# The 64-row remainder of a 576-deep contraction, run as pairs of 64-row array tiles in both gMLP input projections

## The chip, the cores and the metric

The kernel runs on one core of one Trainium2 chip. The metric is the device time of one execution in microseconds (us), and lower is better. A profile's span is the same execution seen by the profiler from the first to the last instruction; it is 1 to 2 us shorter than the time. A few words used throughout: a bank is a piece of PSUM, the memory into which TensorE writes; a chunk is a slice of the contraction, 128 deep (the last one 64), and a unit is a slice of the output columns. PE is TensorE's matrix multiply, PEld its weight load, DVE is VectorE, ACT is ScalarE, POOL is GpSimd and SP is SyncE.

## The reference, cut to what matters

Four layers run in the order A, B, A, B on x of 2048 rows and D = 576 columns. Layer A is local attention with 32 heads, layer B a gMLP. The change is in layer B, and in the layernorm that feeds both kinds.

```python
def _B_ref(x, w_in, w_sp, b_sp, w_out):          # x: (1, 2048, 576); w_in: (576, 4608)
    Fh = w_in.shape[-1] // 2                      # 2304
    z = _gelu(jnp.einsum('bsd,df->bsf', x, w_in)) # both input projections, 576 deep
    z1 = z[..., :Fh].copy()
    z2 = _layernorm(z[..., Fh:], axis=-1)
    g = jnp.einsum('ts,bsf->btf', w_sp, z2) + b_sp[None, :, None]
    return jnp.einsum('bsf,fd->bsd', z1 * g, w_out)
# ...
x = x + _A_ref(_layernorm(x, axis=-1), A_wqkv, A_wo)
x = x + _B_ref(_layernorm(x, axis=-1), B_w_in, B_w_sp, B_b_sp, B_w_out)
# ... and both once more
```

The contraction of both input projections is 576 = 4 x 128 + 64 deep. The second half of `w_in` ("win2" below) makes z2, the first half ("w1") makes z1.

## The kernel before: the parts that matter

The kernel runs the 64-row remainder as a fifth 128-deep matmul in which rows 64 to 127 of the weights are zeros. So it costs as much as a full one: ten w1 matmuls, two of them remainders, take 2.16 us, 216 ns each (chain of waits below).

The normalised rows are written into a buffer of 640 columns, whose last 64 columns were zeroed once, and a DMA transpose puts them into `xnT` as five chunks of 128 partitions.

```python
        for b in self.xn_bufs:
            nc.gpsimd.memset(b[:, D:640], 0.0)
# ...
    def ln_xn(self, x_t, nrows, mv, rstd, nmr, eng="act"):
        # ...
        if eng == "act":
            nc.scalar.activation(out=xn[:nrows, 0:D], in_=x_t[:nrows, :], func=ACT.Identity,
                                 scale=rstd[:nrows, 0:1], bias=nmr[:nrows, 0:1])
        else:
            e = nc.gpsimd if eng == "pool" else nc.vector
            e.tensor_scalar(out=xn[:nrows, 0:D], in0=x_t[:nrows, :], scalar1=mv[:nrows, 0:1],
                            scalar2=rstd[:nrows, 0:1], op0=ALU.subtract, op1=ALU.mult)
        return xn
```

The win2 projection of layer B, for each of 16 blocks of 128 rows: five units (four of 512 columns, one of 256), five chunks each.

```python
        nc.vector.memset(win2b[64:128, 4 - NPF, :].bitcast(i32), 0)
        # ... weights arrive by DMA; chunks 0 to NPF-1 are already resident, the others come late
        def p1_main(i):
            # ...
            if i == 0:
                order = [(u, c) for c in range(NPF) for u in units] + [(u, c) for u in units for c in range(NPF, 5)]
            else:
                order = [(u, c) for u in units for c in range(5)]
            for ((ci, c0, sub, w), c) in order:
                nc.tensor.matmul(pzvs[ci][:, sub * 512:sub * 512 + w], lhsT=self.xnT[:, c, PADL + i * P:PADL + (i + 1) * P],
                                 rhs=win2(c)[:, c0 + sub * 512:c0 + sub * 512 + w],
                                 start=(c == 0), stop=(c == 4))
            # ... gelu on ACT, sum of squares on DVE and ACT, then p1_norm: six slices on DVE, three on POOL
```

The w1 projection with the gating, for each of 18 groups of 128 columns per layer (9 weight blocks x 2), so 36 groups in all:

```python
        for jj in range(NB):
            w1 = p2.tile([P, 5, 256], bf16, name="w1")
            nc.gpsimd.memset(w1[64:128, 4, :], 0.0)
            for c in range(5):
                kc = 128 if c < 4 else 64
                self.dma(w1[:kc, c, :], self.B_w_in[c * P:c * P + kc, jj * 256:(jj + 1) * 256], eng=nc.sync)
            # ...
            for sub in range(2):
                z1T = p2.tile([P, S], bf16, name="z1T")
                for q2 in range(0, NQ, 2):
                    # ...
                    for qq in range(nq2):
                        for c in range(5):
                            nc.tensor.matmul(pz1[:, qq, :], lhsT=w1[:, c, sub * P:(sub + 1) * P],
                                             rhs=self.xnT[:, c, PADL + (q2 + qq) * 512:PADL + (q2 + qq + 1) * 512],
                                             start=(c == 0), stop=(c == 4))
                    # ... gelu on ACT
                for q in range(NQ):
                    pg = self.PT_tile([P, 512], f32, "pg")
                    for i in range(NS):
                        nc.tensor.matmul(pg[:, :], lhsT=z2b[jj][:, i, sub * P:(sub + 1) * P],
                                         rhs=W_sb[:, i, q * 512:(q + 1) * 512],
                                         start=(i == 0), stop=(i == NS - 1))
                    # ... add the bias and multiply by z1T on DVE
```

The softmax here doesn't subtract the row's maximum and nothing guards it: scores larger than these inputs give would overflow.

Of the kernel before, what the change touches and what calls it, by code (L numbers as in the profile page):

```python
# [10 lines left out]
ACT = mybir.ActivationFunctionType  # L11
# [4 lines left out]
i32 = mybir.dt.int32  # L16
# [3 lines left out]
P = 128  # L20
D = 576
# [6 lines left out]
PADL = HALO  # L28
# [33 lines left out]
class K:  # L62
# [24 lines left out]
    def setup(self):  # L87
        nc, tc, cfg, ctx = self.nc, self.tc, self.cfg, self.ctx
# [3 lines left out]
        c = self.consts  # L92
# [32 lines left out]
        for b in self.xn_bufs:  # L125
            nc.gpsimd.memset(b[:, D:640], 0.0)
# [45 lines left out]
    def ln_xn(self, x_t, nrows, mv, rstd, nmr, eng="act"):  # L172
        nc = self.nc
        xn = self.xn_bufs[self.xn_rr % len(self.xn_bufs)]
        self.xn_rr += 1
        if eng == "act":
            nc.scalar.activation(out=xn[:nrows, 0:D], in_=x_t[:nrows, :], func=ACT.Identity,
                                 scale=rstd[:nrows, 0:1], bias=nmr[:nrows, 0:1])
        else:
            e = nc.gpsimd if eng == "pool" else nc.vector  # L180
            e.tensor_scalar(out=xn[:nrows, 0:D], in0=x_t[:nrows, :], scalar1=mv[:nrows, 0:1],  # L181
                            scalar2=rstd[:nrows, 0:1], op0=ALU.subtract, op1=ALU.mult)
        return xn
# [15 lines left out]
    NPF = 3  # L199
# [548 lines left out]
    def layer_B(self, li):  # L748
        nc, tc, cfg = self.nc, self.tc, self.cfg
        S, NS, Fh, NJ, NB, NQ = cfg.S, cfg.NS, cfg.Fh, cfg.NJ, cfg.NB, cfg.NQ  # L750
# [12 lines left out]
        NPF = self.NPF  # L763
# [4 lines left out]
        nc.vector.memset(win2b[64:128, 4 - NPF, :].bitcast(i32), 0)  # L768
        for c in range(NPF, 5):
            kc = 128 if c < 4 else 64  # L770
            self.dma(win2b[:kc, c - NPF, :], self.B_w_in[c * P:c * P + kc, Fh:2 * Fh], eng=(nc.sync, nc.scalar)[c % 2])

        def win2(c):
            return win2a[:, c, :] if c < NPF else win2b[:, c - NPF, :]
# [5 lines left out]
        c0 = 0  # L780
# [9 lines left out]
        def p1_main(i):  # L790
            zp = p1.tile([P, Fh], bf16, name="zp", bufs=2)
            sums = p1.tile([P, ncch + 2], f32, name="z_sums", bufs=3)
            pzvs = []
# [13 lines left out]
            if i == 0:  # L807
                order = [(u, c) for c in range(NPF) for u in units] + [(u, c) for u in units for c in range(NPF, 5)]
            else:
                order = [(u, c) for u in units for c in range(5)]  # L810
            for ((ci, c0, sub, w), c) in order:
                nc.tensor.matmul(pzvs[ci][:, sub * 512:sub * 512 + w], lhsT=self.xnT[:, c, PADL + i * P:PADL + (i + 1) * P],  # L812
                                 rhs=win2(c)[:, c0 + sub * 512:c0 + sub * 512 + w],
                                 start=(c == 0), stop=(c == 4))
# [66 lines left out]
        for jj in range(NB):  # L881
            w1 = p2.tile([P, 5, 256], bf16, name="w1")
            nc.gpsimd.memset(w1[64:128, 4, :], 0.0)
# [5 lines left out]
            for sub in range(2):  # L889
                z1T = p2.tile([P, S], bf16, name="z1T")  # L890
                for q2 in range(0, NQ, 2):
                    nq2 = min(2, NQ - q2)
                    pz1 = self.H_tile("pz1")
                    for qq in range(nq2):
                        for c in range(5):
                            nc.tensor.matmul(pz1[:, qq, :], lhsT=w1[:, c, sub * P:(sub + 1) * P],
                                             rhs=self.xnT[:, c, PADL + (q2 + qq) * 512:PADL + (q2 + qq + 1) * 512],
                                             start=(c == 0), stop=(c == 4))
                    nc.scalar.activation(out=z1T[:, q2 * 512:(q2 + nq2) * 512],
                                         in_=pz1[:, 0:nq2, :].rearrange("p a b -> p (a b)"), func=ACT.Gelu_apprx_tanh)  # L900
# [154 lines left out]
```

## Time and profile before

| | before |
|---|---|
| time, median of 3 runs | 1349.56 us (1348.8 to 1353.09) |
| span of the profile | 1348.4 us |
| PE busy | 1249.9 us, 93% of the span |
| share of PE in the chain of waits that ended last | 62% |
| stage (a), w1 and gating, from the last normalised slice to the first output matmul | 325.7 and 321.5 us in the two B layers |
| one round of a w1 group and its 64 `pg` matmuls | 18.130 us |
| stage (b), win2 with gelu and layernorm: one block | 5.01 us |

The page of the profile gives the busy time of each engine and, in its part 4, the chain that ended last.

```profile
PE 1249.9 (93%) x8656; PEld 659.5 (49%) x8656; DVE 616.5 (46%) x1402; ACT 384.2 (28%) x595; POOL 356.4 (26%) x487
PE 62%; DVE 11%; POOL 10%; issue 7%; DMA 6%; ACT 3%; SPq 1%; ACTq 0%; POOLq 0%; DVEq 0%
```

PE is busy nearly all the time, but only 62% of the chain is PE: in the rest of the time some other engine decides when things go on, although PE has work in between. So the average says little, and the kernel has to be read stage by stage. The table of busy time by stretches does that. This is the kernel before over one pass of stage (b) and one of stage (a); the columns are the stretch, its length, the busy time of each engine with its instructions, PE's granted clock, the share of the DMA engines, and GB/s.

```profile
core 0: us, PE busy (x) PEld busy (x) DVE busy (x) ACT busy (x) POOL busy (x), PEclk, DMA share, GB/s
190.00:286.00 96.00, 87.04 (x430) 41.35 (x427) 67.97 (x210) 55.81 (x129) 69.73 (x85) 1.00 0.56 122
286.00:607.00 321.00, 318.31 (x1474) 144.13 (x1474) 99.49 (x145) 36.87 (x36) 3.57 (x10) 1.00 0.03 9
```

In the second stretch, stage (a), PE is busy 318 of 321 us and nothing else is near a limit: a matmul saved there is time saved. In the first, stage (b), no engine is full. The chain of waits in stage (a) of the kernel before (start, length, what):

```profile
297.07 2.16 PE pz_4181 L896 x10
299.23 2.16 PE pz_4193 L896 x10
301.39 13.81 PE pg L904 x64
315.20 2.16 PE pz_4294 L896 x10
```

Ten w1 matmuls take 2.16 us, so one 512-column matmul takes 216 ns, and the 64 `pg` matmuls say the same (13.81 / 64). One round is 315.20 - 297.07 = 18.13 us.

The Trainium skill, "TensorE: Matmul & The Clock Gate", section "Back-to-back issue gap", gives 131 ns for a sustained stream of 512-column matmuls with weight loads between them, and 216 ns for isolated ones. This trace is such a stream, with a weight load for each matmul (1474 of each in the second stretch above), and shows 216 ns. The measurement decides here: a matmul removed from stage (a) is worth 216 ns.

In stage (b) the timeline (start, length, engine, line, operation, and in brackets the idle time before it and what ended it) shows a loop. These lines are of the kernel before, one block and the start of the next:

```profile
228.25 1.02 ACT L816 ACTIVATE zp<-pz 128x1024 bf16<-128x1024 f32 x1 [1.55 <-POOL z2b_3101 L845]
...
231.10 2.13 POOL L845 TENSOR_SCALAR z2b_3101<-zp,z_rstd,z_nmr 128x256 bf16<-128x256 bf16 x1
231.10 1.77 DVE L819 CUSTOM_DVE_ANT_0 z_junkD<-zp 128x1536 bf16<-128x1536 bf16 x1
...
233.26 1.02 ACT L816 ACTIVATE zp<-pz 128x1024 bf16<-128x1024 f32 x1 [1.56 <-POOL z2b_3101 L845]
```

The first gelu of each block waits 1.55 us for POOL's last normalised slice, and the next block starts 233.26 - 228.25 = 5.01 us later. PE's work per block is 20 x 0.216 + 5 x 0.109 = 4.86 us, less than the period: PE waits for ACT to free its output banks.

### The profile page before, as it was taken

What the parts mean: (1) busy time and instruction counts of PE and PEld (TensorE: products, weight loads), DVE (VectorE), ACT (ScalarE), POOL (GpSimd) and SP (SyncE); (2) the same over time, 40 slices, a digit from 0 to 9 for tenths busy, and PEclk for the clock granted to TensorE, in tenths of its full rate; (3) what the DMA queues carried; (4) which work ended last, traced back from release to release, by engine and by line L of the source; (5) the groups of instructions that cost most, each with busy time, mean ns of one, the idle gap of its engine ahead of it and who ended that gap; (6) DMA issues with size and microseconds to landing.
All of it is one profiled execution on the core that took longest, in us unless ns stands there. A gap on an engine that the chain in (4) does not pass through costs nothing.

```text
span 1348.4 us, 21451 instructions
## 1 busy us (share of the span) xinstructions
PE 1249.9 (93%) x8656; PEld 659.5 (49%) x8656; DVE 616.5 (46%) x1402; ACT 384.2 (28%) x595; POOL 356.4 (26%) x487
## 2 busy tenths in 40 slices
PE   1999969989999999998998987899999999999997
PEld 0456644434444444445754655444444444444576
DVE  4468858843322332332534878588323223333221
ACT  2556726620011111001126665465101111100000
POOL 7445547830000000002141646488000000000111
PEclk9999989999999999997999999899999999999999
DMA  9449759020000000009653677861100000000232
GB/s 264 98 94 145 121 134 214 1 90 6 9 10 9 10 9 9 0 4 266 179 137 62 151 145 129 181 125 41 43 9 9 10 9 9 2 7 1 72 113 67
DMA packets 180128, 101.04 MB, mean 75 GB/s; under 512 B 138276, under 2 KB 162212, under 8 KB 180028
## 3 DMA queue, kind: packets, MB, share of 16 engines
q1 hardware_dynamic: 170208, 84.15, 28.1%
q10 hardware_dynamic: 6364, 8.55, 2.2%
q0 software_dynamic: 3456, 6.96, 2.2%
q8 instruction: 68, 1.11, 0.3%
q14 instruction: 32, 0.26, 0.1%
HBM read 41.16 MB, written 16.52 MB: 43 GB/s over the span
## 4 chain that ended last, share of the span: by engine, by line
PE 62%; DVE 11%; POOL 10%; issue 7%; DMA 6%; ACT 3%; SPq 1%; ACTq 0%; POOLq 0%; DVEq 0%
PE pg L904 36%; PE po L941 9%; DVE z_junkD L819 4%; PE pp L412 3%; DMA QK<-stg 2%; POOL ln_xn_84 L181 2%; POOL ln_xn_81 L181 1%; POOL ln_rstd L164 1%; POOL z_rstd L835 1%; POOL ln_xn_83 L181 1%; POOL ln_xn_82 L181 1%; DMA wout_b<-in_B_w_out_dram 1%; DMA wv_sb<-in_A_wqkv_dram 1%; DMA win2b<-in_B_w_in_dram 1%; DVE z_msq L828 1%
## 5 line engine op out<-in xcount | busy, mean ns | idle before, releaser
L908 DVE TENSOR_TENSOR g_tmp<-pg,bsp 128x512 f32<-128x512 f32 x144 | 99.4, 692 | 435.5 <-PE pg L904 423.9
L412 PE MATMUL pp<-xnT,wqk_sb 128*128 128x512 bf16 x400 | 100.7, 394 | 29.8 <-DMA xnT<-ln_xn_84 28.5
L812 PEld LDWEIGHTS <-xnT 128*128 128x128 bf16 x800 | 78.4, 98 | 97.0 <-issue 13.0
L812 PE MATMUL pz<-win2a,xnT 128*128 128x512 bf16 x384 | 103.1, 379 | 5.9 <-ACT zp L816 4.4
L164 POOL TENSOR_TENSOR ln_rstd<-ln_rstd,neg_half 112x1 f32<-112x1 f32 (+2 forms) x70 | 43.4, 621 | 152.3 <-DVE ln_rstd L163 152.1
L812 PE MATMUL pz<-win2b,xnT 128*128 128x512 bf16 x256 | 77.0, 386 | 6.9 <-DMA win2b<-in_B_w_in_dram 6.9
L816 ACT ACTIVATE zp<-pz 128x1024 bf16<-128x1024 f32 x64 | 65.0, 1020 | 44.6 <-POOL z2b_9746 L845 18.9
L412 PEld LDWEIGHTS <-wqk_sb 128*128 128x128 bf16 x400 | 36.9, 100 | 71.2 <-issue 36.0
L819 DVE CUSTOM_DVE_ANT_0 z_junkD<-zp 128x1536 bf16<-128x1536 bf16 x32 | 56.9, 1777 | 18.7 <-ACT zp L816 18.7
L370 PE MATMUL pv<-wv_sb,xnT 128*128 128x288 bf16 (+1 forms) x380 | 62.2, 286 | 0.2 <-DVE stg L418 0.2
L76 POOL DMA_DIRECT2D wout_b<-in_B_w_out_dram x14 | 7.5, 541 | 172.4 <-PE pg L904 172.4
L76 POOL DMA_DIRECT2D QK<-stg x52 | 31.5, 608 | 73.0 <-ACT stg L420 28.0
L584 DVE TENSOR_TENSOR x_new<-pw,xo 112x288 f32<-112x288 f32 (+1 forms) x76 | 33.5, 445 | 18.0 <-PE pw L582 10.7
L420 ACT CAST stg<-pp 128x512 bf16<-128x512 f32 x54 | 31.0, 585 | 37.4 <-PE pp L412 22.7
L370 PEld LDWEIGHTS <-xnT 128*128 128x128 bf16 (+1 forms) x380 | 33.5, 97 | 15.8 <-issue 1.4
L489 PE MATMUL L_ps<-QK 18*128 18x112 bf16 (+1 forms) x1216 | 32.0, 210 | 4.9 <-DMA QK<-stg 1.7
L418 DVE CAST stg<-pp 128x512 bf16<-128x512 f32 x26 | 18.0, 691 | 37.0 <-PE pp L412 33.5
L159 DVE BATCH_NORM_STATS2 ln_st<-x_new 112x6 f32<-112x288 f32 (+1 forms) x76 | 33.9, 449 | 1.2
L489 PEld LDWEIGHTS <-QK 18*128 18x128 bf16 (+1 forms) x1216 | 20.4, 93 | 25.6 <-issue 21.6
L845 POOL TENSOR_SCALAR z2b_3101<-zp,z_rstd,z_nmr 128x256 bf16<-128x256 bf16 x16 | 32.4, 2024 | 0.0
L845 POOL TENSOR_SCALAR z2b_9746<-zp,z_rstd,z_nmr 128x256 bf16<-128x256 bf16 x16 | 32.4, 2023 | 0.0
L904 PE MATMUL pg<-W_sb,z2b_3093 128*128 128x512 bf16 x128 | 28.4, 379 | 1.9 <-DVE z2b_3093 L848 1.9
(549 smaller groups left out, 2513.3 us busy)
## 6 DMA issues: line engine op xcount, KB each, us to landing
xres_73<-x_new SPq DMA_DIRECT2D x18, 252.0 KB
xo<-xres_74 SPq DMA_DIRECT2D x18, 252.0 KB
xres_75<-x_new SPq DMA_DIRECT2D x18, 252.0 KB
QK<-stg POOLq DMA_DIRECT2D x52, 72.0 KB, 3.8
win2a<-in_B_w_in_dram SPq DMA_DIRECT2D x2, 1728.0 KB
QK<-stg SPq DMA_DIRECT2D x48, 72.0 KB
wqk_sb<-in_A_wqkv_dram ACTq DMA_DIRECT2D x4, 576.0 KB
out_dram<-ob SPq DMA_DIRECT2D x16, 144.0 KB
```

Source lines behind the costliest of these rows:

```text
L164: nc.gpsimd.tensor_tensor(out=rstd[:nrows, :], in0=rstd[:nrows, :], in1=self.neg_half[:nrows, :], op=ALU.pow)
L181: e.tensor_scalar(out=xn[:nrows, 0:D], in0=x_t[:nrows, :], scalar1=mv[:nrows, 0:1], scalar2=rstd[:nrows, 0:1], op0=ALU.subtract, op1=ALU.mult)
L370: nc.tensor.matmul(pv[:nk, 0:288], lhsT=self.xnT[:, c, QT * t:QT * t + nk], rhs=wv_sb[:, c, hh * 288:(hh + 1) * 288], start=(c == 0), stop ...
L412: nc.tensor.matmul(pp[:, :], lhsT=wqk_sb[:, c, wc0:wc0 + P], rhs=self.xnT[:, c, col0:col0 + 512], start=(c == 0), stop=(c == 4))
L489: nc.tensor.matmul(L_ps[:nk, j, ftl * QT:ftl * QT + nq], lhsT=kT[32 * j:32 * j + DH, g, QT * t:QT * t + nk], rhs=qT[32 * j:32 * j + DH, g, ...
L812: nc.tensor.matmul(pzvs[ci][:, sub * 512:sub * 512 + w], lhsT=self.xnT[:, c, PADL + i * P:PADL + (i + 1) * P], rhs=win2(c)[:, c0 + sub * 5 ...
L816: nc.scalar.activation(out=zp[:, c0:c0 + cn], in_=pzvs[ci][:, 0:cn], func=ACT.Gelu_apprx_tanh, accum_out=sums[:, ci:ci + 1])
L819: nc.vector.tensor_tensor_reduce(out=junkD[:], in0=zp[:, 0:SQ_D], in1=zp[:, 0:SQ_D], scale=1.0, scalar=0.0, op0=ALU.mult, op1=ALU.add, acc ...
L845: nc.gpsimd.tensor_scalar(out=z2b[b][:, i, :], in0=zp[:, b * 256:(b + 1) * 256], scalar1=rstd[:, 0:1], scalar2=nmr[:, 0:1], op0=ALU.mult, ...
L904: nc.tensor.matmul(pg[:, :], lhsT=z2b[jj][:, i, sub * P:(sub + 1) * P], rhs=W_sb[:, i, q * 512:(q + 1) * 512], start=(i == 0), stop=(i == ...
L908: nc.vector.tensor_tensor(out=tmp[:], in0=pg[:, :], in1=bsp[:, q * 512:(q + 1) * 512], op=ALU.add)
L941: nc.tensor.matmul(acc[hh], lhsT=uT[j // 2][:, j % 2, i * P:(i + 1) * P], rhs=wout_j(j)[:, hh * 288:(hh + 1) * 288], start=(j == 0), stop= ...
```

## The change

The intent is to split the array into two tiles of 64 rows that work side by side (`tile_position` in the code names the tile). Then two 64-deep remainders, of two different output units, should take the time of one full matmul. One tile takes its operands from partitions 0 to 63 and the other from 64 to 127. So the weights' 64 rows are loaded twice by DMA, and each normalised tile carries its last 64 columns twice, by a small copy before the transpose. The zeroing falls away. The order of the matmuls is changed so that the remainders of a group stand together: two units' full chunks, then all remainders, then the other units' full chunks.

```diff
-        for b in self.xn_bufs:
-            nc.gpsimd.memset(b[:, D:640], 0.0)
@@ ln_xn @@
+            nc.scalar.copy(out=xn[:nrows, D:640], in_=xn[:nrows, 512:D])
         else:
             # ...
+            e.tensor_copy(out=xn[:nrows, D:640], in_=xn[:nrows, 512:D])
@@ layer_B, win2 @@
-        nc.vector.memset(win2b[64:128, 4 - NPF, :].bitcast(i32), 0)
+        self.dma(win2b[64:128, 4 - NPF, :], self.B_w_in[512:576, Fh:2 * Fh], eng=nc.scalar)
@@ p1_main @@
-            # ... the order of before, resident chunks first in block 0
+            def z_full(us, cs):
+                # ... full chunks of units us, start=(c == 0), stop=False
+            def z_half(us):
+                for u in us:
+                    ci, c0, sub, w = units[u]
+                    r = 64 * (u % 2)
+                    nc.tensor.matmul(pzvs[ci][:, sub * 512:sub * 512 + w],
+                                     lhsT=self.xnT[r:r + 64, 4, PADL + i * P:PADL + (i + 1) * P],
+                                     rhs=win2(4)[r:r + 64, c0 + sub * 512:c0 + sub * 512 + w],
+                                     start=(u >= 2), stop=(u < 2), tile_position=(r, 0))
+            z_full(range(2), range(4))
+            z_half(range(nu))
+            # ... then chunks 0 to 3 of units 2, 3, 4
@@ layer_B, w1 @@
-            nc.gpsimd.memset(w1[64:128, 4, :], 0.0)
+            self.dma(w1[64:128, 4, :], self.B_w_in[512:576, jj * 256:(jj + 1) * 256], eng=nc.sync)
@@ w1 group @@
+                def z1_half(q, first):
+                    r = 64 * (q % 2)
+                    nc.tensor.matmul(pz1s[q // 2][:, q % 2, :], lhsT=w1[r:r + 64, 4, sub * P:(sub + 1) * P],
+                                     rhs=self.xnT[r:r + 64, 4, PADL + q * 512:PADL + (q + 1) * 512],
+                                     start=first, stop=not first, tile_position=(r, 0))
+                z1_full(0, True)
+                z1_full(1, True)
+                for q in range(NQ):
+                    z1_half(q, q >= 2)
+                z1_full(2, False)
+                z1_full(3, False)
```

More of the change, by code (lines that the diff above doesn't have):

```diff
@@ L806, in p1_main @@
                     units.append((ci, c0, sub, w))
-            if i == 0:
-                order = [(u, c) for c in range(NPF) for u in units] + [(u, c) for u in units for c in range(NPF, 5)]
-            else:
-                order = [(u, c) for u in units for c in range(5)]
-            for ((ci, c0, sub, w), c) in order:
-                nc.tensor.matmul(pzvs[ci][:, sub * 512:sub * 512 + w], lhsT=self.xnT[:, c, PADL + i * P:PADL + (i + 1) * P],
-                                 rhs=win2(c)[:, c0 + sub * 512:c0 + sub * 512 + w],
-                                 start=(c == 0), stop=(c == 4))
+            def z_full(us, cs):
+                for u in us:
+                    ci, c0, sub, w = units[u]
+                    for c in cs:
+                        nc.tensor.matmul(pzvs[ci][:, sub * 512:sub * 512 + w],
+                                         lhsT=self.xnT[:, c, PADL + i * P:PADL + (i + 1) * P],
+                                         rhs=win2(c)[:, c0 + sub * 512:c0 + sub * 512 + w],
+                                         start=(c == 0), stop=False)
+            def z_half(us):
+                for u in us:
+                    ci, c0, sub, w = units[u]
+                    r = 64 * (u % 2)
+                    nc.tensor.matmul(pzvs[ci][:, sub * 512:sub * 512 + w],
+                                     lhsT=self.xnT[r:r + 64, 4, PADL + i * P:PADL + (i + 1) * P],
+                                     rhs=win2(4)[r:r + 64, c0 + sub * 512:c0 + sub * 512 + w],
+                                     start=(u >= 2), stop=(u < 2), tile_position=(r, 0))
+            nu = len(units)
+            z_full(range(2), range(4))
+            z_half(range(nu))
+            for u in range(2, nu):
+                ci, c0, sub, w = units[u]
+                for c in range(4):
+                    nc.tensor.matmul(pzvs[ci][:, sub * 512:sub * 512 + w],
+                                     lhsT=self.xnT[:, c, PADL + i * P:PADL + (i + 1) * P],
+                                     rhs=win2(c)[:, c0 + sub * 512:c0 + sub * 512 + w],
+                                     start=False, stop=(c == 3))
             for ci, (c0, cn) in enumerate(cchunks):
@@ L890, in layer_B, with z1_full @@
                 z1T = p2.tile([P, S], bf16, name="z1T")
-                for q2 in range(0, NQ, 2):
-                    nq2 = min(2, NQ - q2)
-                    pz1 = self.H_tile("pz1")
-                    for qq in range(nq2):
-                        for c in range(5):
-                            nc.tensor.matmul(pz1[:, qq, :], lhsT=w1[:, c, sub * P:(sub + 1) * P],
-                                             rhs=self.xnT[:, c, PADL + (q2 + qq) * 512:PADL + (q2 + qq + 1) * 512],
-                                             start=(c == 0), stop=(c == 4))
-                    nc.scalar.activation(out=z1T[:, q2 * 512:(q2 + nq2) * 512],
-                                         in_=pz1[:, 0:nq2, :].rearrange("p a b -> p (a b)"), func=ACT.Gelu_apprx_tanh)
+                pz1s = [self.H_tile("pz1") for _ in range(NQ // 2)]
+                def z1_full(q, first):
+                    for c in range(4):
+                        nc.tensor.matmul(pz1s[q // 2][:, q % 2, :], lhsT=w1[:, c, sub * P:(sub + 1) * P],
+                                         rhs=self.xnT[:, c, PADL + q * 512:PADL + (q + 1) * 512],
+                                         start=(first and c == 0), stop=(not first and c == 3))
+                def z1_half(q, first):
[9 more added lines that the diff above has]
+                z1_full(3, False)
+                for q2 in range(0, NQ, 2):
+                    nc.scalar.activation(out=z1T[:, q2 * 512:(q2 + 2) * 512],
+                                         in_=pz1s[q2 // 2][:, :, :].rearrange("p a b -> p (a b)"), func=ACT.Gelu_apprx_tanh)
                 for q in range(NQ):
```

## The prediction

> **What bounds the kernel now.** The table of busy time by stretches shows three kinds of stage. (a) Gating with the w1 projection (286 to 607, 948 to 1266 us): PE is busy 318 of 321 us. The chain of waits repeats: two pieces of ten w1 matmuls, 2.16 us each, then 64 `pg` matmuls, 13.81 us; a 512-column matmul costs 216 ns. (b) The win2 projection with gelu and layernorm (190 to 286, 850 to 948 us): the timeline repeats every 5.01 us. PE needs 20 x 0.216 + 5 x 0.109 = 4.86 us, but ACT's gelu waits 1.56 us for POOL's last normalised slice, and DVE (`z_junkD` 1.77 us plus six slices) and POOL (2.12 us for that slice) feed each other in a loop that sets the period. (c) Attention: POOL waits 2.9 us per tile for DVE; PE does not bind.
>
> **Removed.** Per w1 group two 512-column passes (432 ns), per win2 block also two; the fifth, 256-column unit has no partner.
>
> **Added: switches between full array and row tiles.** The Trainium skill, "TensorEngine Tiling (Array Packing)", Key Properties, says that changing tiling mode drains TensorE. The trace agrees in attention's 18-row tiles: from the start of a 512-column matmul to the first tile takes 312 ns instead of 216, from a 288-column one 218 instead of 122, from the last 112-column tile to the full array 140 instead of about 47. So about 95 ns per switch, 190 a round trip. Row tiles do overlap: 16 tiles of 112 columns start within 195 ns, four passes.
> w1 group: 4.32 us before; after 16 x 0.216 + 2 x 0.216 + 0.02 + 0.19 = 4.10 us. Gain 0.22 us, x36 = 7.9 us, all critical.
> win2 block: the instruction order puts four halves together and the fifth elsewhere, so two round trips: -0.43 + 0.38 = -0.05 us of PE, off the critical path.
>
> **Losses (estimates from the trace).**
> - Start of (b): the first block no longer runs all resident chunks first. PE waits there for win2b already (3.6 and 2.9 us), and a table load (1.28 us) hides part. A third win2b transfer and a later last transpose: 0.7 us x2.
> - Start of (a): a sixth w1 transfer goes first in its queue; an issue takes 0.47 us (five: 2.35): 0.5 us x2.
> - 64-column copies: ACT about 0.22 us (256 columns take 0.38, 1024 take 1.02), POOL about 0.3 us (1 column 0.27, 256 columns 0.6). In the first layer's head and at last tiles: 1 us; by contention on DVE 0.5 us.
> Together about 4 us. The removed memsets were hidden.
>
> **Predicted time:** 1349.6 - 7.9 + 4 = about 1345 us, range 1340 to 1352. Faster by over 2%: 0.01; within: 0.97; slower by over 2%: 0.02.
>
> **What the profile would show.** Each w1-plus-`pg` round shrinks from 18.13 to about 17.91 us; the second half of a pair starts within about 20 ns of the first; about 310 ns from the last full matmul to the first half. (b)'s 5.01 us and attention's 5.8 us per tile stay.
>
> **What would make it wrong.** If the halves don't overlap, 0.43 us more per group turn the gain into an 8 us loss. If 64-row tiles switch more cheaply, the gain is up to 15 us. If POOL's copies stretch DVE in attention (36 tiles), some us are lost. If the new order in (b) makes PE wait for PSUM buffers, its period grows, x32 blocks.

## The result, and the profile after

Ratios in this document are computed as the mean time of one kernel's fast runs over the mean of the other's fast runs of the same rounds, so they are not quite the ratios of the medians quoted beside them. Brackets after a ratio are its 95% interval.

| | before | after |
|---|---|---|
| median of the runs of this comparison | 1351.07 us (1348.8 to 1353.09, 4 runs) | 1343.91 us (1342.94 to 1345.92, 4 runs) |
| ratio, after over before | | 0.9957 [0.9935, 0.998] |
| span of the profile | 1348.4 us | 1341.8 us |
| round of a w1 group and 64 `pg` | 18.130 us | 17.910 us |
| block of stage (b) | 5.01 us | 5.01 us |

The changed kernel is correct and 0.4% faster, which is "within 2%". The prediction was 1345 us in a range of 1340 to 1352.

```profile
PE 1243.5 (93%) x8656; PEld 636.1 (47%) x8656; DVE 614.1 (46%) x1400; ACT 391.4 (29%) x622; POOL 362.6 (27%) x508
```

PE has as many matmuls as before (a remainder is still one instruction) and 6.4 us less busy time. The chain of waits in stage (a) of the changed kernel:

```profile
973.27 1.73 PE pz L914 x8
975.00 0.54 PE pz L920 x4
975.54 1.83 PE pz L914 x8
977.37 13.81 PE pg L935 x64
```

The four remainders, line 920, take 0.54 us from the first one's start to the start of the next full matmul, instead of 4 x 0.216 = 0.86 us. The whole group is 4.10 us instead of 4.32. The timeline shows the starts of the same group's records (a record's length includes the matmul's own latency, so starts are what is compared):

```profile
973.11 1.89 PE L914 MATMUL pz<-xnT,w 128*128 128x512 bf16 x8
974.93 0.60 PE L920 MATMUL pz<-xnT,w 64*128 64x512 bf16 x4
975.47 1.90 PE L914 MATMUL pz<-xnT,w 128*128 128x512 bf16 x8
```

Inside these groups the records' starts repeat to 1 or 2 ns in all rounds: from the last full matmul to the first remainder 312 ns, to its pair partner 3 ns, to the next pair 223 ns, and from the last remainder to the next full matmul 308 ns. A full matmul follows another after 216 ns. So a change of the array's mode costs 312 - 216 = 96 ns on the way in and 308 - 216 = 92 ns on the way out, about 0.19 us for the round trip, and the pairs overlap fully.

These are prices; what fills the 96 ns the runs do not settle. The changed kernel's trace adds one hint. Inside a stream a weight load is recorded 2 ns after the start of the previous matmul, some 214 ns ahead of its own. At the switch the first remainder's load is recorded 308 ns after the start of the last full matmul and only 4 ns ahead of its own. So no load runs ahead across the switch here, and no run here separates the lost lead of the load (it takes 92 ns itself) from an emptying of the array.

The Trainium skill, "TensorEngine Tiling (Array Packing)", Key Properties, says that changing the tiling mode drains TensorE but gives no figure; these 96 and 92 ns are this kernel's figure. "TensorE: Matmul & The Clock Gate", Part 3, puts the tiles of a pack about 4 ns apart at issue; the trace has 3 ns.

In stage (b) the same lines as before, in the changed kernel:

```profile
224.68 1.02 ACT L835 ACTIVATE zp<-pz 128x1024 bf16<-128x1024 f32 x1 [1.56 <-POOL z2b L864]
...
227.67 0.61 PE L820 MATMUL pz<-win2b,xnT 64*128 64x512 bf16 x4
228.11 0.27 PE L820 MATMUL pzs<-win2b,xnT 64*128 64x256 bf16 x1
...
229.70 1.02 ACT L835 ACTIVATE zp<-pz 128x1024 bf16<-128x1024 f32 x1 [1.56 <-POOL z2b L864]
...
230.86 0.81 PE L811 MATMUL pz<-win2a,xnT 128*128 128x512 bf16 x3 [0.21 <-ACT zp L835]
```

All five remainders of the block stand together (lines at 227.67 and 228.11), with one round trip through the modes. PE's work is 16 x 0.216 + 4 x 0.109 for the full chunks, 2 x 0.216 + 0.109 for the remainders and 0.19 for the switches, 4.62 us instead of 4.86. But the gelu still waits 1.56 us for POOL and comes 229.70 - 224.68 = 5.02 us after the last one, and what PE saved turns into a wait of its own: the idle 0.21 us before the next block, for ACT. The 0.24 us are saved off the critical path, in the 28 of 32 blocks whose remainders stand together, and are worth nothing.

At the start of stage (b) time was lost. The first block of the first B layer, before and then after:

```profile
188.06 1.02 PE L812 MATMUL pz<-win2a,xnT 128*128 128x512 bf16 x4 [0.99 <-DVE x_new L584]
...
195.01 1.68 PE L812 MATMUL pz<-win2b,xnT 128*128 128x512 bf16 x7 [3.64 <-DMA win2b<-in_B_w_in_dram]
...
197.20 1.02 ACT L816 ACTIVATE zp<-pz 128x1024 bf16<-128x1024 f32 x1
```

```profile
193.13 1.44 PE L811 MATMUL pz<-win2a,xnT 128*128 128x512 bf16 x3 [0.54 <-DVE x_new L584]
197.07 0.58 PE L811 MATMUL pz<-win2b,xnT 128*128 128x512 bf16 x1 [2.50 <-DMA win2b<-in_B_w_in_dram]
...
200.69 1.01 PE L820 MATMUL pz<-win2b,xnT 64*128 64x512 bf16 x2 [1.32 <-DMA win2b<-in_B_w_in_dram]
...
204.13 1.02 ACT L835 ACTIVATE zp<-pz 128x1024 bf16<-128x1024 f32 x1
```

From the first win2 matmul to the first gelu it is 9.1 us before and 11.0 after: PE stops twice for late weights, with less resident work done in between. The clock differs as well. These are the two stretches, columns as in the table by stretches (before, then after):

```profile
188.06:197.20 9.14, 5.50 (x30) 2.76 (x30) 1.80 (x4) 1.28 (x2) 4.52 (x3) 1.00 0.53 138
193.13:204.13 11.00, 7.17 (x17) 1.97 (x17) 0.77 (x3) 1.28 (x1) 3.57 (x5) 0.50 0.75 168
```

The granted clock was 1.00 before and 0.50 after, and full matmuls that follow each other start 427 ns apart after the change, 215 before. The last wait for weights ends only 0.6 us later after the change (7.55 us after the first win2 matmul against 6.95); the other 1.3 us pass between it and the gelu. In all five traces with the change's win2 part the clock in this stretch is 0.50 to 0.74, in the eight with win2 as before 0.77 to 1.00. No run separates the clock from the order of the matmuls.

The lines of the first block show one thing more: the stage begins 5 us later after the change (193.13 against 188.06). That time went in the attention layer before it. There the first full set of 16 score tiles of the attention comes late. From the timeline of PE, before and then after:

```profile
51.39 0.22 PE L489 MATMUL L_ps<-QK 18*128 18x112 bf16 x2
...
53.39 0.38 PE L489 MATMUL L_ps<-QK 18*128 18x112 bf16 x16
```

```profile
58.91 0.22 PE L489 MATMUL L_ps<-QK 18*128 18x112 bf16 x1
...
60.88 0.38 PE L489 MATMUL L_ps<-QK 18*128 18x112 bf16 x16 [0.17 <-ACT P_sb L508]
```

So the result has one gain of about the predicted size, and losses at the edges of stages whose cause the result alone does not tell.

### The profile page after: what moved, and what is told of

Read it like the earlier page. It is cut to its first block, busy times and chain, and to the rows that moved or that the text cites. A ratio compares the mean times of both kernels' runs of the same rounds, so it can differ in the third digit from the quotient of the medians.

```text
span 1341.8 us, 21436 instructions
## 1 busy us (share of the span) xinstructions
PE 1243.5 (93%) x8656; PEld 636.1 (47%) x8656; DVE 614.1 (46%) x1400; ACT 391.4 (29%) x622; POOL 362.6 (27%) x508
## 5 line engine op out<-in xcount | busy, mean ns | idle before, releaser
L935 PE MATMUL pg<-W_sb,z2b 128*128 128x512 bf16 x2304 | 505.8, 380 | 2.2 <-DVE z2b L867 2.2
L935 PEld LDWEIGHTS <-z2b 128*128 128x128 bf16 x2304 | 226.1, 98 | 274.6 <-DVE z2b L867 2.7
L914 PE MATMUL pz<-xnT,w 128*128 128x512 bf16 x576 | 136.9, 380 | 2.6 <-DMA w<-in_B_w_in_dram 2.6
L972 PEld LDWEIGHTS <-uT 128*128 128x128 bf16 x1152 | 114.4, 99 | 42.9 <-issue 10.6
L972 PE MATMUL po<-wout_b,uT 128*128 128x288 bf16 x864 | 117.2, 293 | 9.4 <-DMA wout_b<-in_B_w_out_dram 9.4
L940 DVE TENSOR_TENSOR uT<-g_tmp,z1T 128x512 bf16<-128x512 f32 x144 | 99.5, 692 | 14.7 <-ACT z1T L930 4.8
L864 POOL TENSOR_SCALAR z2b<-zp,z_rstd,z_nmr 128x256 bf16<-128x256 bf16 x96 | 103.7, 1091 | 3.6 <-POOL z_nmr L856 0.4
L180 POOL TENSOR_SCALAR ln_xn<-x_new,ln_mv,ln_rstd 112x576 bf16<-112x576 f32 (+1 forms) x38 | 95.7, 2518 | 3.9
L527 DVE TENSOR_TENSOR P_sb<-P_sb,mask_base 128x1792 bf16<-128x1792 bf16 (+1 forms) x76 | 81.1, 1067 | 12.9 <-ACT P_sb L508 12.7
L505 ACT ACTIVATE P_sb<-L_ps 128x896 bf16<-128x896 f32 (+1 forms) x88 | 74.1, 870 | 35.9 <-PE O_ps L540 17.4
L582 PE MATMUL pw<-wo_sb,oT 128*128 128x288 bf16 x380 | 58.9, 300 | 10.5 <-DMA oT<-o_t 8.7
```

The lines of the kernel that those rows point to most:

```text
L505: nc.scalar.activation(out=P_sb[:nk, 2 * hh:2 * hh + 2, :, 0:nq], in_=Lv[:nk, 2 * hh:2 * hh + 2, :, 0:nq], func=ACT.Exp, scale=float(scale))
L527: nc.vector.tensor_tensor(out=Pv[:nk, :, 0:nq], in0=Pv[:nk, :, 0:nq], in1=m[:nk, None, 0:nq].to_broadcast([nk, 16, nq]), op=ALU.mult)
L864: nc.gpsimd.tensor_scalar(out=z2b[b][:, i, :], in0=zp[:, b * 256:(b + 1) * 256], scalar1=rstd[:, 0:1], scalar2=nmr[:, 0:1], op0=ALU.mult, ...
L914: nc.tensor.matmul(pz1s[q // 2][:, q % 2, :], lhsT=w1[:, c, sub * P:(sub + 1) * P], rhs=self.xnT[:, c, PADL + q * 512:PADL + (q + 1) * 512 ...
L940: nc.vector.tensor_tensor(out=u[:, sub, q * 512:(q + 1) * 512], in0=tmp[:], in1=z1T[:, q * 512:(q + 1) * 512], op=ALU.mult)
L972: nc.tensor.matmul(acc[hh], lhsT=uT[j // 2][:, j % 2, i * P:(i + 1) * P], rhs=wout_j(j)[:, hh * 288:(hh + 1) * 288], start=(j == 0), stop= ...
```

## The experiments

The theory to test: (T1) stage (a) gains 0.22 us per group because pairs overlap and a round trip costs 0.19 us; (T2) stage (b) gives nothing back, since its loop over ACT, POOL and DVE is untouched, and its first block loses; (T3) the copies cost a little by themselves, in attention. The rivals: (R1) the gain comes from somewhere else, for example from less weight loading or from the removed zeroing, and not from pairs; (R2) the win2 part gains too; (R3) the losses in attention come from scatter, or from the win2 part, not from the copies.

Twelve experiments ran on the chip, all with correct results: ten new kernels, and the changed kernel and the kernel before once more. They ran in four series, each on one chip with its own runs of the kernel before:

| series | kernel before, median (range, 11 runs) |
|---|---|
| 1 | 1346.5 us (1342.04 to 1350.16) |
| 2 | 1347.77 us (1345.52 to 1351.67) |
| 3 | 1347.54 us (1344.38 to 1352.36) |
| 4 | 1347.65 us (1346.22 to 1348.75) |

### The changed kernel again

No edit: the changed kernel ran again beside its parts, so that all are compared on one chip.

> The changed kernel once more, as the yardstick of this series. Both theories: ratio to before 0.993 to 0.997. In its trace the stage table of two traces so far shows the gating stages shorter by 3.4 and 4.5 us, the first attention layer longer by 4.8 us and the second shorter by 3.1 us. Theory 'schedule': the longer first attention layer (head plus 4.8 us) comes back in every trace of this program. Rival 'noise': it scatters by some us from trace to trace, and comes back smaller or with the other sign.

Measured: 1345.63 us, ratio 0.9995 [0.9978, 1.0011]. Both theories had expected 0.993 to 0.997 and missed: on this chip the whole change gains nothing that can be told from zero. The rounds are 17.910 us, as in the first trace. The first attention layer is again longer than in the kernel before, by 3.5 us (166.4 against 162.9; a table of all traces follows below), as theory 'schedule' said, though less than its 4.8 us. The first win2 block takes 10.4 and 10.5 us to the first gelu, where the first trace has 11.0 and 10.5. So the rounds repeat exactly, the start of a stage moves by some tenths of a us, and the total moves by some us between series and runs, in the kernel before as well as after. What makes it move is left open.

### Only the w1 part

```diff
@@ kernel before, plus the copies in ln_xn, plus @@
-            nc.gpsimd.memset(w1[64:128, 4, :], 0.0)
+            self.dma(w1[64:128, 4, :], self.B_w_in[512:576, jj * 256:(jj + 1) * 256], eng=nc.sync)
# ... and the w1 group of the change (z1_full, z1_half); win2 stays as before
```

> Pairs in the w1 projection alone, copies kept, win2 projection as before. Theory (the gain is all in the w1 groups, 0.22 us x36 = 7.9 us, and the win2 pairs are worth nothing): as fast as the changed kernel or about 1 us faster, about 1343 us, ratio to before near 0.994. Rival (part of the gain comes from the win2 stage): slower than the changed kernel by 2 us or more.

Measured: 1341.93 us, ratio 0.997 [0.995, 0.9989]. That is less than the 0.994 expected, but faster than the whole change in the same series (its six runs lie between 1340.23 and 1344.42, those of the whole change between 1344.10 and 1347.37). The start of stage (b) stays short, 9.5 and 9.4 us to the first gelu. So the part in stage (a) carries the gain, and the part in stage (b) takes some of it away.

### Only the win2 part

```diff
@@ kernel before, plus the copies in ln_xn, plus @@
-        nc.vector.memset(win2b[64:128, 4 - NPF, :].bitcast(i32), 0)
+        self.dma(win2b[64:128, 4 - NPF, :], self.B_w_in[512:576, Fh:2 * Fh], eng=nc.scalar)
# ... and z_full, z_half in p1_main; w1 stays as before
```

> Pairs in the win2 projection alone, copies kept, w1 projection as before. Theory: the DVE and POOL loop sets the 5.01 us period, so no gain; copies and the later start cost 1 to 6 us: 1352 to 1357 us. Rival (PE sets the pace there too): 32 blocks x 0.24 us = 7.7 us faster than the copies alone.

Measured: 1353.0 us, ratio 1.0051 [1.0031, 1.0071]: slower. R2 falls. The time from the first win2 matmul to the first gelu is 11.0 and 10.2 us, against 9.1 and 9.6 in the kernel before. That is 2.5 us of the 6.9 us that the ratio stands for (0.0051 x 1347); the copies account for about 1.5 (next run), and the rest, some 3 us, is not placed. Stage (a), which this kernel has as before, is 0.9 us longer in its trace than in the first trace of before (327.6 + 320.5 against 325.7 + 321.5 us), and two traces of the kernel before differ by 1.0 us there (647.2 and 648.2 in sum), so that is no explanation.

### Only the copies

```diff
-        for b in self.xn_bufs:
-            nc.gpsimd.memset(b[:, D:640], 0.0)
+            nc.scalar.copy(out=xn[:nrows, D:640], in_=xn[:nrows, 512:D])
+            e.tensor_copy(out=xn[:nrows, D:640], in_=xn[:nrows, 512:D])
```

Both matmul parts stay as before: the doubled columns meet zeros in the weights.

> Only the 64-column copies after each layernorm, both projections as before (the weights' upper rows stay zero, so the result is right). Theory 'schedule': the copies and the new instruction order they bring lengthen the first attention layer by about 4 us: 1353 to 1356 us. As predicted blind (1.5 us in all): 1352 to 1353 us. Rival 'noise': within 1 us of before.

Measured: 1348.36 us, ratio 1.0012 [0.9995, 1.003]. By time alone this can't be told from nothing; the 4 us more that theory 'schedule' expected of the total did not come. The trace tells more. Its set of 16 score tiles comes as late as in the changed kernel (timeline of PE, copies only):

```profile
59.68 0.38 PE L489 MATMUL L_ps<-QK 18*128 18x112 bf16 x16 [0.18 <-ACT P_sb L508]
```

A copy itself is small; this is one on POOL in the changed kernel:

```profile
181.81 0.24 POOL L182 COPY ln_xn<-ln_xn 112x64 bf16<-112x64 bf16 x1
```

To see whether the shift is scatter, the duration of the two attention stages was read in all fourteen traces: six without copies (two of the kernel before, one of its reordering, and the three kernels below that get the second half by a DMA) and eight with them:

| stage | without copies: mean (range) | with copies: mean (range) | difference |
|---|---|---|---|
| first A layer: first matmul to first win2 matmul | 163.8 us (162.6 to 165.0) | 167.5 us (166.4 to 168.4) | +3.6 us |
| second A layer: last output matmul to first win2 matmul | 160.1 us (158.8 to 162.2) | 158.0 us (156.4 to 159.4) | -2.1 us |

In the first layer the ranges do not touch, so R3 falls for it: the copies cost 3.6 us there. In the second they overlap slightly and the copies gain about 2.1 us. The net is 1.5 us. A kernel with the copies also has its instructions in another order in this layer (the score tiles come one by one, where they came in twos), and which of the two, the copy's 0.24 us or the new order, makes the 3.6 us has not been separated.

### The kernel before, a second trace

No edit: one look at the kernel before, to know how much a trace of the same kernel moves.

> The kernel before once more, for a second trace of it, to compare stage by stage: so far one trace of it stands against five of kernels with copies. Theory 'the copies and the order they bring lengthen the first attention layer by 3 to 5 us': first matmul to first win2 matmul again about 163 us (with copies 166.4 to 168.4). Rival 'noise': 165 us or more here.

Measured: one run of 1355.04 us (state unknown, so its total is not used), span 1353.3. The round is 18.130 us again, to the nanosecond; the first block of stage (b) takes 9.0 and 9.5 us, and the first A layer 164.7 us where the first trace has 162.9. That lies between the theory's 163 and the rival's 165 and decides nothing by itself; the table above, with all traces, does. So a round can be compared between single traces to some ns, an attention stage only to some 2 us, and the start of (b) to some tenths (0.1 us between these two traces, but 0.6 us between the two of the changed kernel).

### The w1 part without copies

The second half of the activations is not made by copies; one DMA per layer copies the finished remainder from partitions 0 to 63 to 64 to 127.

```diff
         p1_norm(NS - 1)
+        self.dma(self.xnT[64:128, 4, PADL:PADL + S], self.xnT[0:64, 4, PADL:PADL + S], eng=nc.scalar)
# ... and the w1 part of the change; win2 and ln_xn stay as before
```

> Pairs in the w1 projection alone, and no copies at the layernorms: one transfer inside on-chip memory makes the second copy of the 64 rows after the win2 stage. The attention layers then have the instruction order of before. Theory: the pairs' 7.2 us of the traces come whole, less 1 to 2 us at the start of the gating stage: ratio to before 0.995 to 0.9965, and 1 to 4 us faster than w1_only, with 163 us for the first attention layer. Rival (the copies cost nothing): as w1_only, 0.997.

Measured: 1347.17 us, ratio 0.9988 [0.997, 1.0005], less gain than the expectation had. The attention part came out as the theory says: the score tiles are back to where they were in the kernel before (timeline of PE, this kernel),

```profile
54.01 0.38 PE L489 MATMUL L_ps<-QK 18*128 18x112 bf16 x16
```

the first A layer takes 163.6 us, and the rounds are 17.910 us. But stage (a) is 323.5 and 322.5 us, where the kernel with copies and the w1 part has 321.6 and 317.2: 7.2 us were lost in it. The first w1 matmul comes 5.04 us after the last normalised slice in both layers, against 2.04 and 2.15 us in the kernel before, and 35 `pg` matmuls run ahead of it in both (33 and 45 in the kernel before, 36 and 48 in the changed one). So the stage starts badly here. Whether the added DMA does that, or the different order in front of it, was not tried. Taking the copies away in this form gained nothing over keeping them.

### Every matmul of stage (a) as row-tile pairs

If a round trip costs 0.19 us and pairs overlap fully, a stage that never leaves the 64-row mode saves two passes of 216 ns per group with no switch. Each 128-deep matmul of w1 and `pg` becomes two 64-deep ones, on both tiles, for two output units at a time; the second phase swaps the tiles. The activations come by DMA as in the last kernel.

```diff
+                for q in (0, 2):
+                    for c in range(4):
+                        z1_part(q, c, 0, c == 0, False)        # lower tile
+                        z1_part(q + 1, c, 64, c == 0, False)   # upper tile
+                    z1_part(q, 4, 0, False, False)             # the remainder
+                    fz[q] = fence(z1_part(q + 1, 4, 64, False, False))
+                for q in (0, 2):
+                    for c in range(4):
+                        m1 = z1_part(q + 1, c, 0, False, c == 3)   # tiles swapped
+                        m2 = z1_part(q, c, 64, False, c == 3)
+                        # ... both after fz[q]
# ... the same for pg, with four banks
```

The Trainium skill, "TensorEngine Tiling (Array Packing)", Restrictions and Gotchas, Gotcha 1, warns that different row tiles can't access one PSUM bank simultaneously and that software must synchronise. So a fence was put in, a tiny ACT copy that waits for the first phase's last matmul. No run here shows what the chip would do without it.

> As w1_dma, but all matmuls of the gating stage, w1 and pg alike, run as pairs of 64-row tiles, so that the array never switches inside the stage. If the two switches of 95 ns are what halves the gain, each round takes 4 x 4.5 x 0.216 + 13.81 = 17.70 us instead of 17.91 (before 18.13): another 7.5 us faster than w1_dma, ratio to before about 0.990. Rival (the lost half is not the switches but the halves themselves, or twice the matmuls cost issue time): not faster than w1_dma.

Measured: 1345.93 us, ratio 0.9987 [0.9975, 0.9999]. The round is 17.698 us, 432 ns below before, which is two passes exactly. The chain of waits of this kernel:

```profile
302.85 3.88 PE pz L902 x36
306.73 13.81 PE pg L933 x128
```

Thirty-six 64-deep matmuls take 3.88 us, 18 passes of 216 ns, and 128 halves of `pg` take the 13.81 us that 64 full ones took. So the rate is the same and no switch is left. But 36 rounds x 0.432 = 15.6 us should have been gained, and stage (a) is 324.7 and 322.3 us, only 0.2 us less in sum than in the first trace of before. The timeline at the stage's start shows where they went:

```profile
286.36 6.56 PE L902 MATMUL pz<-xnT,w 64*128 64x512 bf16 x36 [6.09 <-DMA w<-in_B_w_in_dram]
```

PE stands idle for 6.09 us until the first w1 weights come; only 36 `pg` halves, 18 passes, ran ahead of them, where in the kernel before 33 full `pg` matmuls did. After the wait the same 36 halves take 6.56 us instead of 3.88; the granted clock is 0.60 from 286.36 to 292.75 us and 1.00 in the group at 302.85. So the gain inside the rounds was given back in a new wait at the edge and in a slow group behind it. If that is the reason, `pg` put first must bring the gain back; that was tried below.

### Resident chunks first in the first win2 block

```diff
+            if i == 0:
+                order = [(u, c) for c in range(NPF) for u in range(nu)] + [(u, 3) for u in range(nu)]
+                # ... these full chunks first, then all remainders, start=False, stop=True
+            else:
+                # ... as in the change
```

This is the changed kernel with the order of before restored in the first block alone, to test what that order costs.

> The changed kernel, except that the first win2 block of each layer again runs all resident chunks first, as before, and its remainder last. The traces show the first gelu 10.4 to 11.0 us after the first win2 matmul in kernels with win2 pairs, 8.3 to 9.6 without. Theory (the order of the first block is that loss): gelu back at about 9.5 us, 2 to 3 us faster than the changed kernel in all, ratio to before about 0.998 of this series. Rival (the third win2b transfer delays it): no change.

Measured: 1344.18 us, ratio 0.997 [0.9958, 0.9982]. The first gelu comes 9.8 and 10.2 us after the first win2 matmul. Over all traces the two kinds of kernel compare so:

| first win2 matmul to first gelu | win2 as before, 8 traces | win2 of the change, 5 traces | difference of the means | this kernel |
|---|---|---|---|---|
| first B layer | 9.5 us (9.0 to 10.3) | 10.9 us (10.4 to 11.0) | +1.4 us | 9.8 us |
| second B layer | 9.7 us (8.3 to 10.9) | 10.5 us (10.2 to 10.9) | +0.8 us | 10.2 us |

So by this one trace the order in the first block explains most of the loss in the first layer, and little of the smaller one in the second, where the ranges overlap anyway. The granted clock in this stretch is 0.98 and 0.82 here, so the order and the clock came back together. The time itself was not compared with the changed kernel in the same rounds and does not decide this.

### Two round trips per w1 group

The halves of two units stand after those units' own full chunks, so a group has two pairs, each with its own round trip.

```diff
                 z1_full(1, True)
-                for q in range(NQ):
-                    z1_half(q, q >= 2)
-                z1_full(2, False)
-                z1_full(3, False)
+                z1_half(0, False)
+                z1_half(1, False)
+                z1_full(2, True)
+                z1_full(3, True)
+                z1_half(2, False)
+                z1_half(3, False)
```

> The changed kernel with the four halves of a w1 group in two pairs, so the array goes to 64-row tiles and back twice per group. Theory (a switch costs about 95 ns): each round of w1 group and pg takes 17.91 + 0.19 = 18.10 us, as in before; 36 x 0.19 = 6.8 us slower than the changed kernel. Rival (the drain is hidden or the 95 ns belong to the first tile's weight load only once): 17.91 us and no slower.

Measured: 1354.55 us, ratio 1.0049 [1.0023, 1.0075]. The round is 18.123 us. Timeline of PE:

```profile
521.75 1.89 PE L914 MATMUL pz<-xnT,w 128*128 128x512 bf16 x8
523.57 0.39 PE L920 MATMUL pz<-xnT,w 64*128 64x512 bf16 x2
523.89 1.90 PE L914 MATMUL pz<-xnT,w 128*128 128x512 bf16 x8
525.73 0.39 PE L920 MATMUL pz<-xnT,w 64*128 64x512 bf16 x2
...
539.87 1.89 PE L914 MATMUL pz<-xnT,w 128*128 128x512 bf16 x8
```

From 521.75 to 539.87 it is 18.12 us, that is the round of before to 0.01 us: the second round trip eats the whole 0.22 us that pairing gained. The measured price of the second trip, 18.123 - 17.910 = 0.213 us, confirms 0.19 within 0.02 us; the changed kernel's one trip, against the all-pairs kernel above, costs nearly the same, 17.910 - 17.698 = 0.212 us. As this kernel has lost its gain in (a) and keeps all losses of the copies and the win2 part, it is slower than before.

### The same remainders, both on one tile

```diff
                 def z1_half(q, first):
-                    r = 64 * (q % 2)
+                    r = 0
```

Here the mode, the order and the round trip are those of the change, but all four halves of a w1 group go to the same tile, one after the other.

> The changed kernel with all four halves of a w1 group on the lower 64 rows, so that they cannot overlap. Theory (the gain is that two halves stream at once): starts of halves 216 ns apart in place of 3 and 223, each round 17.91 + 2 x 0.216 = 18.34 us, 36 x 0.43 = 15.5 us slower than the changed kernel and 8 us slower than before. Rival (a 64-row matmul is itself cheaper than a 128-row one): rounds near 17.9 us.

Measured: 1361.27 us, ratio 1.0097 [1.0074, 1.0121], the slowest of all. The round is 18.340 us. Timeline of PE:

```profile
523.77 1.89 PE L914 MATMUL pz<-xnT,w 128*128 128x512 bf16 x8
525.59 1.03 PE L920 MATMUL pz<-xnT,w 64*128 64x512 bf16 x4
...
542.11 1.89 PE L914 MATMUL pz<-xnT,w 128*128 128x512 bf16 x8
```

The four halves take 1.03 us where the pairs took 0.60, so pairing is worth 18.340 - 17.910 = 0.430 us per group, two passes, and a 64-deep matmul alone is no cheaper than a 128-deep one. R1 falls: with the same zeroing removed and the same loads, the gain is gone without the pairs.

### Stage (a) in row-tile pairs, first gating matmuls first

The kernel with all of stage (a) in pairs lost its gain in a wait for the first weights. The `pg` matmuls do not need them, so in the first group of a layer they are put first, and the multiplication with z1T after both.

```diff
+                first = jj == 0 and sub == 0
+                if not first:
+                    z1_all()
                 # ... pg pairs; tmps[qq] = pg + bias
+                        if not first:
+                            gate(qq)
+                if first:
+                    z1_all()
+                    for qq in range(NQ):
+                        gate(qq)
```

> best64 with the first round's pg matmuls ahead of its w1 group. The trace of best64 has the rounds at 17.69 us as expected, but its gating stages last 324.7 and 322.3 us from the last normalised slice to the first output matmul, against 325.6 and 321.5 before: its first round waits 6 us for the first w1 transfer, which starts only when the normalised slices are done, and then runs its 36 halves in 6.6 us in place of 3.9. Theory (the start of the stage, not the rounds, took the gain back): 7 us less in each of the two stages, about 14 us faster than best64, ratio to before about 0.988. Rival (the time is bound elsewhere, at the stage's end or by DVE): no faster than best64.

Measured: 1332.65 us (1330.16 to 1336.16, 6 runs), ratio 0.9892 [0.9872, 0.9912]. This beats both kernels: its slowest run is below the fastest of the kernel before (1344.38 in the same series) and below the fastest that the changed kernel ever showed (1342.94). The rounds are 17.698 us as in the last form, and the stage is 316.4 and 314.1 us, against 325.7 and 321.5: 16.7 us less in sum, where 15.6 were worked out for the rounds alone. Timeline of PE at the start of the stage:

```profile
282.69 10.75 PE L943 MATMUL pg<-W_sb,z2b 64*128 64x512 bf16 x98 [1.96 <-DVE z2b L855]
293.28 4.05 PE L902 MATMUL pz<-xnT,w 64*128 64x512 bf16 x36
```

The wait of 6.09 us is gone; PE works on `pg` while the weights arrive.

### The kernel before, with first gating matmuls first

The same reordering on the kernel before, to see how much of the last result is the order and how much the tiles.

```diff
+                first = jj == 0 and sub == 0
+                if not first:
+                    z1_all()          # the ten-matmul pieces of before
                 # ... pg as before, tmps[q] = pg + bias
+                if first:
+                    z1_all()
```

> The kernel before, full array throughout, with only the first round's pg matmuls ahead of its w1 group: the last part of best64_pgfirst alone. From the last normalised slice to the first output matmul, before takes 325.6 and 321.5 us (second trace 325.3 and 322.9), best64_pgfirst 316.5 and 314.1. Theory (the 64-row tiles give 0.43 us a round, 7.8 us a stage, of it, and before's own first round hides its w1 transfer nearly whole, 1 us lost): 1 us a stage, ratio to before 0.998 to 0.999. Rival (most of the 14 us is the reordered first round, and the tiles add little): ratio near 0.993.

Measured: 1346.1 us (1340.87 to 1352.36), ratio 0.998 [0.9963, 0.9996]. The rounds are 18.130 us and the stage is 324.3 and 320.7 us, 2.2 us less in sum than in the first trace of before. So the order is worth about 0.2% by itself; the other 0.9% of the last kernel need the pairs. That kernel also has a fourth bank for `pg`, which was not tried alone; but a round is a full stream of matmuls in both kernels, 84 x 215.8 ns = 18.13 us and 82 x 215.8 ns = 17.70 us, so a free bank more has nothing to shorten inside it.

## Why the prediction was right

The total fell where it was predicted: 1343.91 us against 1345, well inside 1340 to 1352, and "within 2%" had 0.97. The terms, by the traces:

1. **The w1 group: right.** "Gain 0.22 us" per group and "from 18.13 to about 17.91 us": measured 18.130 and 17.910. "About 310 ns from the last full matmul to the first half": 312. "Within about 20 ns of the first": 3 ns. The price of a switch, read before the change from the 18-row tiles of attention (about 95 ns), holds for 64-row tiles, at 96 and 92 ns. The runs with two trips and without pairs show both halves of this sum apart: 0.21 us for one more trip, 0.43 us for the overlap.
2. **Stage (b) is not bound by PE: right.** "(b)'s 5.01 us ... stay": 5.01 us, and the win2 part alone is slower, not faster.
3. **"The instruction order puts four halves together and the fifth elsewhere, so two round trips: -0.43 + 0.38 = -0.05 us of PE": wrong.** In 28 of 32 blocks all five stand together, with one round trip, so PE saved 0.24 us. I had read the order off the first blocks and carried it over to the others. It did not matter for the time, since a wait of 0.21 us for ACT took its place.
4. **Start of (b), "0.7 us x2": mechanism right, size off.** Between the traces with and without the win2 part it is 1.4 us in the first layer and 0.8 in the second, 2.2 instead of 1.4 in sum. The prediction had late weights and their order, which the trace shows; it did not have the granted clock, 0.50 in the first such block against 1.00 before.
5. **Start of (a), "0.5 us x2": not seen as a loss in time.** The first w1 matmul does come later (4.16 and 5.01 us after the last slice, against 2.04 and 2.15), but `pg` matmuls fill in: 36 and 48 run ahead of it, against 33 and 45. The sum of both stages (a) is 639.1 and 640.6 us in two traces of the changed kernel, against 647.2 and 648.2 in two of the kernel before. That is 7.8 us less in the mean, and the rounds should give 36 x 0.22 = 7.9: within the 1.5 us by which two traces of one kernel differ here, nothing was lost at the edge.
6. **Copies, "1 us; by contention on DVE 0.5 us": the sum right, its parts wrong.** The traces show +3.6 us in the first A layer and -2.1 in the second, so 1.5 in all. The estimate of 1.5 us met this by luck: it had no gain in the second layer, and far less loss in the first. The part "by contention on DVE" is not seen: in the first A layer the output projections of successive tiles start 5.73 us apart before and 5.74 after (medians), as "attention's 5.8 us per tile stay" said. The first of them starts at 85.8 us before and 91.7 after, so the loss lies in front of the tiles.

Put together from the traces: -7.8 in (a), +2.2 at the start of (b), +1.5 in attention, so -4.1 us. The two timed comparisons gave -5.8 us (0.0043 x 1351) and -0.7 us (0.0005 x 1347), on either side of it. By their intervals the first lies between -8.8 and -2.7 us, the second between -3.0 and +1.5. So the sum fits the first and not the second, and so does the predicted gain of 4.6 us: that the total came out as predicted was in part the luck of the first comparison. The prediction had added its losses up to about 4 us, and the traces have 2.2 + 1.5 = 3.7, though three of its terms are not what was written. Why the same pair of kernels differs by 5 us between the two series is open (the chip of the first is not on record); so are about 3 us of what the win2 part alone lost, and what exactly the copies do in the first A layer.

## What to carry to other kernels

Before you pack a short remainder into row tiles, price the switch of the array's mode against the passes saved (here 0.19 to 0.21 us a round trip against 0.216 us a pass): one switch per group of four halves pays, one per pair pays nothing, and a whole stage kept in the small tiles pays in full, because two 64-deep tiles together run at the rate of one 128-deep matmul. Do it only in the stage that PE bounds: in the other stage the saved 0.24 us per block became a wait, and its first block, with late weights and a granted clock of 0.50 to 0.74, came 2.2 us later in sum. And after a stage is made faster inside, look at its first few microseconds, where the gain of the all-pairs kernel had gone (6.09 us waiting for weights, and a group at a clock of 0.60 after it) until work that didn't need them was put first.

## What the Trainium skill lacked or had wrong

- "TensorEngine Tiling (Array Packing)", Key Properties, says that a mode switch drains TensorE, without a price. These runs show 96 ns into 64-row tiles and 92 ns out again behind 512-column matmuls, 0.19 us a round trip, and 0.21 us for one more trip in a group.
- "TensorEngine Tiling (Array Packing)", Theoretical Speedup, gives up to 2x for dimensions of at most 64. It lacks one side of it that the runs show: full 128-deep work cut into 64-row pairs loses nothing (128 halves in 13.81 us, as 64 full matmuls), so that a stage can be moved as a whole to avoid the switch.
- "TensorE: Matmul & The Clock Gate", section "Back-to-back issue gap", gives 131 ns per sustained 512-column matmul with weight loads, and calls 216 ns the gap of an isolated one. The streams of stage (a), with their weight loads, show 216 ns (64 in 13.81 us). The point is about the figure of this section alone.
